# First stage on 64x64 quarters, third stage in halves, rows of x and of first-stage results moved as 48 + 48 + 2, and three buffers of third-stage results

## The chip, the cores and the metric

The kernel runs on one core of a Trainium2 chip. The metric is device time in microseconds of one execution. Five engines run side by side, each working its own list of instructions in order: TensorE (PE, with weight loads shown as PEld), VectorE (DVE), ScalarE (ACT), GpSimd (POOL) and SyncE (SP), which here issues all DMAs. They wait for each other by semaphores.

## The reference

```python
X = np.fft.rfft(x, axis=1)                    # x: (8, 3136, 256) f32
Yr = Xr @ w_r - Xi @ w_i + b_r                # Xr, Xi = X.real, X.imag; w: 256x256
Yi = Xr @ w_i + Xi @ w_r + b_i
Y = soft_threshold(Yr, 0.01) + 1j * soft_threshold(Yi, 0.01)
x = np.fft.irfft(Y, n=3136, axis=1)
h = np.maximum(x @ w_in, 0.0)                 # w_in: 256x1024
conv_out = sum(conv_w[k] * shifted(h, k - 1) for k in range(3))
out = (h * sigmoid(conv_out)) @ w_out         # w_out: 1024x256
```

The batch has 8 images of 3136 = 49 x 64 rows.

## The kernel before, in words

The transform of 3136 points is split into 49 times 64. **Stage 1** does the 49-point part: an item is a pair (image, jc), of which there are 8 x 8; `load_x` brings four columns j of 98 rows (49 rows n, and two halves h of the 64, interleaved) into a tile xr of 98x4x256, `stage1` multiplies by f1 (98x98, which holds the same 49-point table for both h) in two f32 matmuls of 512 columns (two half-items), ScalarE copies each from its one bank of PSUM (pool ps1) to a1, and a1 goes to the scratch sc1 in HBM as one DMA of 98 rows. `stage1_head` does the eight items of image 0 ahead of the loop, on tiles of their own (hx, ha). **Stage 2** loads a2 from sc1 (512 KB, `load_a2`) and does the 64-point part for four frequencies u at once; **mix** is the complex product with w_r, w_i, with each f32 operand split into two parts (hi, lo) of a faster type, three matmuls for one, 36 in all; **threshold** is the soft threshold, on ACT, DVE and POOL; **stage 3** is the inverse 64-point part, 12 matmuls into ps_s3, four frequencies in two banks (pool psa), copied by ScalarE in one instruction to z1 (two buffers) and stored to the scratch sc2.

One loop of 50 items (and three turns to drain) runs them as a pipeline: iteration `it` has stage 2 of item it, mix of it-1, threshold of it-2, stage 3 of it-3. The order within an iteration is written out by hand, under `manual_schedule`, for TensorE, VectorE and ScalarE: generators are advanced in turn by `some(generator, n)`. Half-items of stage 1 for the following images are let in by `one(k)` at four places of an iteration. How many is told by `due`, the running total after iteration it: 2, 5, 9, 13, 16, then three more each to 34 at it = 10, then 13 in five iterations until all 112 are done at it = 40. `back(n)` puts steps of a background job between (splitting the feed-forward weights). SP's order and the head are ordered by the compiler's own scheduler.

After the loop, **stage 4** (line 514) is the inverse 49-point part: blocks of 32 f32 matmuls on 64x64 quarters of TensorE's array, with z2 loaded from sc2 by two DMAs a block into three buffers, and results in the two buffers of psh, two banks each. Then follow `up` (line 533), the convolution and gate, and `down` (line 561).

PSUM has eight banks, in this order: ps1 one, ps2 two, psm three, psa two. The pool psh takes the first four again after the loop.

Names in a profile lose their trailing numbers: ps_s is any of ps_s1, ps_s2, ps_s3, ps_s4 (the line tells which), a is a1 or a2, z is z1 or z2, sc is sc1 or sc2.

Of the kernel before, what the change touches and what calls it, by code (L numbers as in the profile page):

```python
# [19 lines left out]
R = 49  # L20
# [15 lines left out]
def _tables():  # L36
# [8 lines left out]
    fwd1 = np.zeros((R, 2, 2 * R))  # L45
    for h in range(2):
        for uu in range(1, U + 1):
            for c in range(2):
                fwd1[:, h, (uu - 1) * 4 + c * 2 + h] = f[:, c, uu]
        fwd1[:, h, 4 * U + h] = f[:, 0, 0]  # L50
# [9 lines left out]
    for uu in range(U + 1):  # L60
# [32 lines left out]
        "fwd1": fwd1.reshape(2 * R, 2 * R).astype(np.float32),  # L93
# [7 lines left out]
def spectral_ffn_kernel(ctx: ExitStack, tc: tile.TileContext, x, w_r, w_i, b_r, b_i,  # L101
# [19 lines left out]
    with ExitStack() as ab:  # L121
# [7 lines left out]
        ps1 = ab.enter_context(tc.tile_pool(name="ps1", bufs=1, space=PSUM))  # L129
# [4 lines left out]
        f1 = c1.tile([K1, P], F32, name="f1")[:, 0:K1]  # L134
# [19 lines left out]
        def load_mix():  # L154

            raw = [stg.tile([P, NT, D], F32, name=f"wm_raw{k}", tag="raw", bufs=2) for k in range(2)]
            for k in range(2):
                ld = nc.sync.dma_start(raw[k], (w_r, w_i)[k].rearrange("(t p) e -> p t e", p=P))
            split(wmix_hi[:, :, 0, :], wmix_lo[:, :, 0, :], raw[1])
# [4 lines left out]
            return ld  # L164
# [77 lines left out]
        def load_x(pool, b, jc, parts=1, **kw):  # L242

            xr = pool.tile([K1, JC, D], F32, name="xr", **kw)
            xv = x[b].rearrange("(n j) d -> n j d", j=H)[:, jc * JC:(jc + 1) * JC, :]
            w = JC // parts
            for k in range(0, JC, w):
                ld = nc.sync.dma_start(xr[:, k:k + w, :], xv[:, k:k + w, :])
            return xr, ld

        def stage1(b, jc, xr):

            a1 = s1p.tile([K1, JC, D], F32, name="a1", bufs=3)
            for j in range(0, JC, 2):
                ps = ps1.tile([K1, 2, D], F32, name="ps_s1")
                nc.tensor.matmul(ps, f1, xr[:, j:j + 2, :], start=True, stop=True)  # L256
                nc.scalar.copy(a1[:, j:j + 2, :], ps)
                if j + 2 == JC:
                    nc.sync.dma_start(sc1[b][:, jc * JC:(jc + 1) * JC, :], a1)
                yield None  # L260

        def stage1_head(xs, b=0):

            with tc.tile_pool(name="ha", bufs=1, reuse_waits="tile") as ha:
                for jc, xr in enumerate(xs):
                    a1 = ha.tile([K1, JC, D], F32, name=f"ha{jc}")
                    for j in range(0, JC, 2):
                        k = (jc * 2 + j // 2) % 4
                        if k < 3:
                            ps = psm.tile([K1, 2, D], F32, name="ps_s1h", tag=f"ps_mx{k}")  # L270
                        else:
                            ps = ps1.tile([K1, 2, D], F32, name="ps_s1")
                        nc.tensor.matmul(ps, f1, xr[:, j:j + 2, :], start=True, stop=True)  # L273
                        if j:
                            nc.vector.tensor_copy(a1[:, j:j + 2, :], ps)
                        else:
                            nc.scalar.copy(a1[:, j:j + 2, :], ps)
                    st = nc.sync.dma_start(sc1[b][:, jc * JC:(jc + 1) * JC, :], a1)
            return st
# [73 lines left out]
        def stage3(b, g, s):  # L353

            sh, sl = s
            ps = psa.tile([KQ, UG, D], F32, name="ps_s3")
            for k in range(UG):
                u = g * UG + k if g < NG else U + k % 2
                for n, (lt, rh) in enumerate(((i1_hi, sh), (i1_hi, sl), (i1_lo, sh))):
                    nc.tensor.matmul(ps[:, k, :], lt[:, u, :], rh[:, k, :], start=(n == 0), stop=(n == 2))  # L360
            z1 = io.tile([KQ, UG, D], F32, name="z1", bufs=2)
            nc.scalar.copy(z1, ps)
# [64 lines left out]
        for it in range(n_it + 3):  # L427
# [28 lines left out]
            one(1)  # L456
# [175 lines left out]
```

## Time and profile before

| | us |
|---|---|
| three runs | 1737.77, 1741.54, 1738.86; median 1738.86 |
| the profiled execution | 1738.14 |
| its span on the core | 1736.3 |
| TensorE busy in the span | 1690.5 (97%) |
| VectorE, ScalarE, GpSimd busy | 1471.0, 1198.4, 118.6 |
| TensorE clock granted, mean | 0.985 of full |

The span is the stretch between the first and the last recorded instruction. A busy TensorE is not one at its peak: the record of a matmul reaches from its start to the end of its results, and neighbours overlap. Durations of matmuls are therefore read from start to start. `<-` after a row's time names what the engine waited for.

### The profile page before, as it was taken

Reading aid. Unit: us, or ns where it says so; the run is one execution under the profiler, and the core shown is the slowest. Engines: PE = TensorE matmul, PEld = TensorE weight load, DVE = VectorE, ACT = ScalarE, POOL = GpSimd, SP = SyncE. Lnnn points to the kernel's source line nnn. Section 1 sums busy time; section 2 is a strip of 40 time slices with the busy share of each in tenths; the row PEclk is TensorE's granted clock in tenths of the full one; section 3 lists DMA queues with packets and bytes.
Section 4 is the critical chain, followed back from the end, with each engine's and each line's share of the span. In section 5 each row is a group of like instructions: output and inputs, shape, how many; then the busy total and the mean of one; then the engine's idle time right before and its main releaser. Section 6 shows DMA issues by size and latency. Waiting matters only on the chain.

```text
span 1736.3 us, 35086 instructions
## 1 busy us (share of the span) xinstructions
PE 1690.5 (97%) x14944; PEld 1552.5 (89%) x14944; DVE 1471.0 (85%) x1757; ACT 1198.4 (69%) x1565; POOL 118.6 (7%) x54
## 2 busy tenths in 40 slices
PE   5999999999997999999999999999999999999999
PEld 2778888888986999999999999999999999999998
DVE  2788988898993988888888898888888888888887
ACT  2567677767663877777777677777777777777776
POOL 0122222222230000000000000000000000000000
PEclk7999999999996999999999999999999999999999
DMA  7877777667435110111111111111101111100001
GB/s 229 256 236 243 229 227 239 223 203 250 142 106 130 39 41 22 31 51 51 52 53 53 38 41 51 51 41 51 51 22 42 51 51 42 51 22 22 22 22 43
DMA packets 134604, 165.87 MB, mean 96 GB/s; under 512 B 9166, under 2 KB 112590, under 8 KB 134448
## 3 DMA queue, kind: packets, MB, share of 16 engines
q1 hardware_dynamic: 134448, 163.62, 30.7%
q8 instruction: 118, 1.93, 0.5%
q14 instruction: 38, 0.31, 0.1%
HBM read 86.01 MB, written 77.59 MB: 94 GB/s over the span
## 4 chain that ended last, share of the span: by engine, by line
PE 93%; DMA 4%; DVE 2%; issue 1%; ACT 1%; SPq 0%; DVEq 0%; ACTq 0%
PE acc L561 32%; PE ps_h L533 32%; PE ps_mx L328 11%; PE ps_s L256 5%; PE ps_s L300 5%; PE ps_s L514 4%; PE ps_s L360 3%; DMA z<-sc 1%; DMA wm_raw<-in_w_i_dram 1%; DMA t<-in_fwd_dram 1%; DVE v L336 0%; DMA sc<-a 0%; PE ps_s1h L273 0%; DMA xr<-in_x_dram 0%; DVE p L332 0%
## 5 line engine op out<-in xcount | busy, mean ns | idle before, releaser
L561 PE MATMUL acc<-wout,gh 128*128 128x256 f32 x3136 | 567.7, 281 | 1.5 <-ACT gh L547 1.5
L533 PE MATMUL ps_h<-yh,win 128*128 128x450 f32 x1792 | 550.4, 368 | 0.0
L542 DVE SCALAR_TENSOR_TENSOR c<-h,cw,c 128x896 f32<-128x896 f32 x448 | 513.4, 1148 | 26.7 <-ACT c L540 24.5
L561 PEld LDWEIGHTS acc<-wout,gh 128*128 128x128 f32 x3136 | 491.3, 188 | 10.4 <-ACT gh L547 1.9
L561 PE MATMUL acc<-wout,gl 128*128 128x256 f32 x1568 | 437.0, 280 | 0.0
L533 PEld LDWEIGHTS ps_h<-yh,win 128*128 128x128 f32 x1792 | 339.2, 189 | 25.8
L535 ACT ACTIVATE h<-ps_h 128x900 f32<-128x900 f32 x224 | 207.1, 925 | 209.9 <-PE ps_h L533 209.9
L533 PE MATMUL ps_h<-yl,win 128*128 128x450 f32 x896 | 329.7, 368 | 0.0
L544 DVE TENSOR_TENSOR c<-h,c 128x896 f32<-128x896 f32 x224 | 243.9, 1089 | 70.1 <-ACT c L543 69.6
L561 PEld LDWEIGHTS acc<-wout,gl 128*128 128x128 f32 x1568 | 293.6, 188 | 0.1
L548 DVE TENSOR_TENSOR gl<-c,gh 128x896 fp32r<-128x896 f32 x224 | 243.2, 1089 | 41.4 <-ACT gh L547 40.5
L547 ACT CAST gh<-c 128x896 fp32r<-128x896 f32 x224 | 211.6, 945 | 60.9 <-DVE c L544 60.5
L543 ACT ACTIVATE c<-c 128x896 f32<-128x896 f32 x224 | 214.0, 955 | 52.8 <-DVE c L542 51.8
L328 PE MATMUL ps_mx<-wmix_hi,fl 128*128 128x256 f32 x600 | 185.1, 308 | 2.7 <-DVE fl L310 2.7
L328 PE MATMUL ps_mx<-wmix_hi,fh 128*128 128x256 f32 x600 | 183.5, 306 | 0.7 <-DVE v L336 0.5
L533 PEld LDWEIGHTS ps_h<-yl,win 128*128 128x128 f32 x896 | 169.6, 189 | 11.1
L540 ACT ACTIVATE c<-h,cw 128x896 f32<-128x896 f32 x168 | 175.1, 1042 | 1.8
L328 PE MATMUL ps_mx<-wmix_lo,fh 128*128 128x256 f32 x600 | 168.4, 281 | 0.0
L350 POOL TENSOR_TENSOR sl<-v,sh 128x1024 fp32r<-128x1024 f32 x50 | 118.4, 2368 | 407.7 <-PE ps_s L360 249.0
L336 DVE TENSOR_TENSOR v<-ps_mx,p 64x512 f32<-64x512 f32 x200 | 137.4, 687 | 2.9
L300 PEld LDWEIGHTS ps_s<-t,a 128*128 128x128 f32 (+1 forms) x800 | 99.4, 197 | 37.0 <-issue 26.3
L328 PEld LDWEIGHTS ps_mx<-wmix_hi,fh 128*128 128x128 f32 x600 | 113.2, 189 | 19.1 <-issue 17.4
(84 smaller groups left out, 1861.0 us busy)
## 6 DMA issues: line engine op xcount, KB each, us to landing
z<-sc SPq DMA_DIRECT2D x128, 200.0 KB
xr<-in_x_dram SPq DMA_DIRECT2D x63, 392.0 KB
a<-sc SPq DMA_DIRECT2D x48, 512.0 KB
sc<-z SPq DMA_DIRECT2D x48, 512.0 KB
out_dram<-o SPq DMA_DIRECT2D x27, 896.0 KB
sc<-a SPq DMA_DIRECT2D x56, 392.0 KB
sc<-ha SPq DMA_DIRECT2D x8, 392.0 KB
win_bits<-in_moe_w_in_dram SPq DMA_DIRECT2D x4, 512.0 KB
```

Source lines behind the costliest of these rows:

```text
L300: nc.tensor.matmul(ps[:, k], a2[0:rows, k, t * P:(t + 1) * P], t2[0:rows, u, :], start=(k == 0), stop=(k == UG - 1), skip_group_check=True)
L328: nc.tensor.matmul(ps[c][:, k, :], lt, rh, start=(n == 0), stop=(n == len(mm) - 1))
L336: nc.vector.tensor_tensor(v[dst, :, k, :], ps[c][src], p1[src, c], op=ALU.add)
L533: nc.tensor.matmul(ps[:, a, 0:CH + 2], lt, rh, start=(n == 0), stop=(n == len(mm) - 1))
L535: nc.scalar.activation(h, ps[:, :, 0:CH + 2], AF.Relu)
L540: nc.scalar.mul(c, h[:, :, 0:CH], cw[:, 0, f:f + 1])
L542: nc.vector.scalar_tensor_tensor(c, h[:, :, k:k + CH], cw[:, k, f:f + 1], c, op0=ALU.mult, op1=ALU.add)
L543: nc.scalar.activation(c, c, AF.Sigmoid)
L544: nc.vector.tensor_tensor(c, h[:, :, 1:CH + 1], c, op=ALU.mult)
L547: nc.scalar.copy(gh, c)
L548: nc.vector.tensor_tensor(gl, c, gh.bitcast(F32), op=ALU.subtract)
L561: nc.tensor.matmul(acc[m // 2][:, m % 2, :], lt[:, sl], rh[:, f, :], start=(f == 0 and n == 0 and m % 2 == 0), stop=(f == NF - 1 and n == ...
```

## The change

- Stage 1 puts the two halves h at partitions 0 to 48 and 64 to 112, with f1 as one 49x64 table for each. An item is four f32 matmuls of 49x64 by 512 columns, one on each quarter of the array (row half h, output half c, where c picks two of the four columns j). The results of h go to a bank of their own (ps1 has two buffers).
- x is loaded as 48 + 48 + 2 rows of 4 KB, three DMAs; a1 is stored as three DMAs, in runs of 2 KB. f1 is loaded as 128x64.
- Whole items take the place of half-items: `due` becomes (due + 1) // 2, and there are two places for them, after the first eight matmuls of mix and at the end of the iteration.
- Stage 3 works two frequencies at a time into one bank (psa one bank), with a copy each; its first half stands amid mix, its second at the end. z1 has three buffers.
- The head's order is written out too: all items of image 0 come ahead of the splitting of the mixing weights.
- The scratch kept for descriptors of DMAs is set to 4096 bytes.

```diff
-        f1 = c1.tile([K1, P], F32, name="f1")[:, 0:K1]
+        f1 = c1.tile([P, P], F32, name="f1")[:, 0:SP]
-        ps1 = ab.enter_context(tc.tile_pool(name="ps1", bufs=1, space=PSUM))
+        ps1 = ab.enter_context(tc.tile_pool(name="ps1", bufs=2, space=PSUM))
...
+        def load_x(pool, b, jc, **kw):
+            xr = pool.tile([P, JC, D], F32, name="xr", **kw)
+            xv = x[b].rearrange("(n h j) d -> h n j d", h=2, j=H)[:, :, jc * JC:(jc + 1) * JC, :]
+            for h in range(2):
+                nc.sync.dma_start(xr[h * SP:h * SP + R - 1], xv[h, 0:R - 1])
+            ld = nc.sync.dma_start(xr[R - 1::SP], xv[:, R - 1])
+            return xr, ld
+        def quarters(ps, xr):
+            for c in range(2):
+                for h in range(2):
+                    rows = slice(h * SP, h * SP + R)
+                    nc.tensor.matmul(ps[h][c * SP:(c + 1) * SP], f1[rows, :], xr[rows, 2 * c:2 * c + 2, :], start=True, stop=True)
+        def store_a1(b, jc, a1):
+            to = sc1[b].rearrange("(w h) (q c j) d -> q c w h j d", h=2, c=2, j=2)[jc]
+            for c in range(2):
+                nc.sync.dma_start(to[c, 0:R - 1], a1[c * SP:c * SP + R - 1])
+            return nc.sync.dma_start(to[:, R - 1], a1[R - 1::SP])
         def stage1(b, jc, xr):
-            a1 = s1p.tile([K1, JC, D], F32, name="a1", bufs=3)
-            for j in range(0, JC, 2):
-                ps = ps1.tile([K1, 2, D], F32, name="ps_s1")
-                nc.tensor.matmul(ps, f1, xr[:, j:j + 2, :], start=True, stop=True)
-                nc.scalar.copy(a1[:, j:j + 2, :], ps)
-                if j + 2 == JC:
-                    nc.sync.dma_start(sc1[b][:, jc * JC:(jc + 1) * JC, :], a1)
-                yield None
+            a1 = s1p.tile([P, 2, JC // 2, D], F32, name="a1", bufs=3)
+            ps = [ps1.tile([P, JC // 2, D], F32, name="ps_s1") for h in range(2)]
+            quarters(ps, xr)
+            for h in range(2):
+                nc.scalar.copy(a1[:, h], ps[h])
+            store_a1(b, jc, a1)
+            yield None
...
         def stage3(b, g, s):
             sh, sl = s
-            ps = psa.tile([KQ, UG, D], F32, name="ps_s3")
-            for k in range(UG):
...
-            z1 = io.tile([KQ, UG, D], F32, name="z1", bufs=2)
-            nc.scalar.copy(z1, ps)
+            z1 = io.tile([KQ, UG, D], F32, name="z1", bufs=3)
+            for h in range(0, UG, 2):
+                ps = psa.tile([KQ, 2, D], F32, name="ps_s3")
+                for k in range(h, h + 2):
...
+                nc.scalar.copy(z1[:, h:h + 2, :], ps)
+                if h == 0:
+                    yield None
...
             with tc.issue_after(ld.ins):
-                load_mix()
+                mix_w = load_mix()
+                next(mix_w)
                 load_t2(0)
-                st = stage1_head(xh)
+                with tc.manual_schedule(engines={mybir.EngineType.PE, mybir.EngineType.DVE, mybir.EngineType.Activation}):
+                    st = stage1_head(xh)
+                    next(mix_w)
...
+            due = (due + 1) // 2
...
-            one(1)
+            one(0)
             some(two, 1)
             some(mx, 5)
...
-            some(mx, 5 if n_a > 3 else 9)
-            one(2)
+            some(mx, 9)
+            some(s3, 1)
             some(th, 1)
-            some(mx, 9)
-            one(3)
             some(mx, 64)
...
-            if 0 <= it - 3 < n_it:
-                stage3(*items[it - 3], ss.pop(it - 3))
-            one(0)
+            some(s3, 1)
+            one(1)
```

How TensorE's list changes, in the middle of the loop. Before, from the end of stage 3 to the first half-item inside mix (ps_mx is mix, ps_s at line 300 is stage 2):

```order
L360 MATMUL ps_s_2527<-sh,i_lo 128x256
L256 MATMUL ps_s_2543<-xr,f_113 98x512
L300 MATMUL ps_s_2552<-t_114,a_2435 128x128 x4
L300 MATMUL ps_s_2561<-t_114,a_2435 128x128 x4
L328 MATMUL ps_mx_2572<-wmix_hi,fh 128x256
L328 MATMUL ps_mx_2572<-wmix_lo,fh 128x256
L328 MATMUL ps_mx_2572<-wmix_hi,fl 128x256
L328 MATMUL ps_mx_2572<-wmix_hi,fh 128x256
L328 MATMUL ps_mx_2572<-wmix_lo,fh 128x256
L328 MATMUL ps_mx_2572<-wmix_hi,fl 128x256
L328 MATMUL ps_mx_2572<-wmix_hi,fh 128x256
L328 MATMUL ps_mx_2572<-wmix_lo,fh 128x256
```

Now, inside mix, from the last mixing matmuls ahead of an item to those behind it:

```order
L337 MATMUL ps_mx_2591<-wmix_hi,fh 128x256
L337 MATMUL ps_mx_2591<-wmix_lo,fh 128x256
L256 MATMUL ps_s_2612<-xr,f_113 64x512
L256 MATMUL ps_s_2613<-xr,f_113 64x512
L256 MATMUL ps_s_2612<-xr,f_113 64x512
L256 MATMUL ps_s_2613<-xr,f_113 64x512
L337 MATMUL ps_mx_2591<-wmix_hi,fl 128x256
```

An item is one group of four, the two h alternating, where single matmuls of 98 rows were spread over the iteration.

At the end of the loop, TensorE's list before, where stage 4 begins (line 514, two blocks interleaved; line 360 is stage 3):

```order
L360 MATMUL ps_s_5711<-sl,i_hi 128x256
L360 MATMUL ps_s_5711<-sh,i_lo 128x256
L360 MATMUL ps_s_5734<-sh,i_hi 128x256
L514 MATMUL ps_s_5817<-i_76,z_5814 64x49
L514 MATMUL ps_s_5855<-i_76,z_5852 64x49 x2
L514 MATMUL ps_s_5817<-i_76,z_5814 64x49
```

And now (stage 4 is line 529, stage 3 line 371, mix line 337):

```order
L337 MATMUL ps_mx_6064<-wmix_lo,fh 128x256
L337 MATMUL ps_mx_6064<-wmix_hi,fl 128x256
L529 MATMUL ps_s_6303<-i_76,z_6300 64x49
L529 MATMUL ps_s_6341<-i_76,z_6338 64x49 x2
L529 MATMUL ps_s_6303<-i_76,z_6300 64x49
L529 MATMUL ps_s_6341<-i_76,z_6338 64x49
```

The first two blocks of stage 4 moved from behind the last mix to ahead of it; the next two stand after 21 of its 36 matmuls, two more behind its end, and the others among the last halves of stage 3.

SP's list in the loop, before and now, for one item of stage 1 (z is z1, a<-sc the load of a2):

```order
L285 DMA a_1312<-sc_1_58 128x4x256
L248 DMA xr<-in_x_dram 98x1024
L259 DMA sc_2_59<-a_1077 98x1024
L248 DMA xr<-in_x_dram 98x1024
L364 DMA sc_0_65<-z_1191 128x1024
```

```order
L294 DMA a_1478<-sc_1_58 128x4x256
L247 DMA xr<-in_x_dram 48x1024 x2
L248 DMA xr<-in_x_dram 2x1024
L262 DMA sc_2_59<-a_1275 96x1x512 x2
L263 DMA sc_2_59<-a_1275 2x2x512
L376 DMA sc_0_65<-z_1306 128x1024
```

Each DMA on this list waits for the landing of the one eight places before it, since eight semaphores are used in turn, and otherwise for its source and target.

More of the change, by code (lines that the diff above doesn't have):

```diff
@@ L44, in _tables @@
     f[:, 1, :] = -np.sin(ang)
[L45 to L50, printed above, removed]
+    fwd1 = np.zeros((2, SP, SP))
+    for uu in range(1, U + 1):
+        for c in range(2):
+            fwd1[:, :R, (uu - 1) * 2 + c] = f[:, c, uu]
+    fwd1[:, :R, 2 * U] = f[:, 0, 0]
     g = np.transpose(f, (1, 2, 0)).copy()
@@ L158, in load_mix @@
                 ld = nc.sync.dma_start(raw[k], (w_r, w_i)[k].rearrange("(t p) e -> p t e", p=P))
+            yield ld
             split(wmix_hi[:, :, 0, :], wmix_lo[:, :, 0, :], raw[1])
@@ L240, in later @@
                 yield from work
[L242 to L248, printed above, removed]
-            return xr, ld
-        def stage1(b, jc, xr):
-            a1 = s1p.tile([K1, JC, D], F32, name="a1", bufs=3)
-            for j in range(0, JC, 2):
-                ps = ps1.tile([K1, 2, D], F32, name="ps_s1")
-                nc.tensor.matmul(ps, f1, xr[:, j:j + 2, :], start=True, stop=True)
-                nc.scalar.copy(a1[:, j:j + 2, :], ps)
-                if j + 2 == JC:
-                    nc.sync.dma_start(sc1[b][:, jc * JC:(jc + 1) * JC, :], a1)
-                yield None
+        def load_x(pool, b, jc, **kw):
[4 more added lines that the diff above has]
+            ld = nc.sync.dma_start(xr[R - 1::SP], xv[:, R - 1])
+            return xr, ld
+        def quarters(ps, xr):
[5 more added lines that the diff above has]
+            to = sc1[b].rearrange("(w h) (q c j) d -> q c w h j d", h=2, c=2, j=2)[jc]
+            for c in range(2):
+                nc.sync.dma_start(to[c, 0:R - 1], a1[c * SP:c * SP + R - 1])
+            return nc.sync.dma_start(to[:, R - 1], a1[R - 1::SP])
+        def stage1(b, jc, xr):
+            a1 = s1p.tile([P, 2, JC // 2, D], F32, name="a1", bufs=3)
[5 more added lines that the diff above has]
+            yield None
         def stage1_head(xs, b=0):
@@ L265, in stage1_head @@
                 for jc, xr in enumerate(xs):
[L266 to L278, printed above, removed]
+                    a1 = ha.tile([P, 2, JC // 2, D], F32, name=f"ha{jc}")
+                    if jc % 2:
+                        ps = [psm.tile([P, JC // 2, D], F32, name="ps_s1h", tag=f"ps_mx{h}") for h in range(2)]
+                    else:
+                        ps = [ps1.tile([P, JC // 2, D], F32, name="ps_s1") for h in range(2)]
+                    quarters(ps, xr)
+                    nc.scalar.copy(a1[:, 0], ps[0])
+                    nc.vector.tensor_copy(a1[:, 1], ps[1])
+                    st = store_a1(b, jc, a1)
             return st
@@ L355, in stage3 @@
             sh, sl = s
-            ps = psa.tile([KQ, UG, D], F32, name="ps_s3")
-            for k in range(UG):
-                u = g * UG + k if g < NG else U + k % 2
-                for n, (lt, rh) in enumerate(((i1_hi, sh), (i1_hi, sl), (i1_lo, sh))):
-                    nc.tensor.matmul(ps[:, k, :], lt[:, u, :], rh[:, k, :], start=(n == 0), stop=(n == 2))
-            z1 = io.tile([KQ, UG, D], F32, name="z1", bufs=2)
-            nc.scalar.copy(z1, ps)
+            z1 = io.tile([KQ, UG, D], F32, name="z1", bufs=3)
+            for h in range(0, UG, 2):
+                ps = psa.tile([KQ, 2, D], F32, name="ps_s3")
+                for k in range(h, h + 2):
+                    u = g * UG + k if g < NG else U + k % 2
+                    for n, (lt, rh) in enumerate(((i1_hi, sh), (i1_hi, sl), (i1_lo, sh))):
+                        nc.tensor.matmul(ps[:, k - h, :], lt[:, u, :], rh[:, k, :], start=(n == 0), stop=(n == 2))
+                nc.scalar.copy(z1[:, h:h + 2, :], ps)
+                if h == 0:
+                    yield None
             if g < NG:
@@ L367, in stage3 @@
                     nc.sync.dma_start(sc2[b + k][:, U, :], z1[:, k, :])
+            yield None
         def some(g, n):
@@ L431, in spectral_ffn_kernel @@
             due = (2, 5, 9, 13, 16)[it] if it < 5 else 16 + 3 * (it - 4) if it <= 10 else 34 + 13 * (it - 10) // 5
+            due = (due + 1) // 2
             n_a, given = due - given, due
+            s3 = stage3(*items[it - 3], ss.pop(it - 3)) if 0 <= it - 3 < n_it else iter(())
             work = 5 <= it < n_it
```

7 lines of the change are left out of this document (3 added, 4 removed).

## The prediction

> **What bounds the kernel now.** I read the engine totals and the chain first, then busy time by stage, then single iterations, then the matmuls of the changed lines one by one, last the transfers.
>
> ```profile
> PE 1690.5 (97%) x14944; PEld 1552.5 (89%) x14944; DVE 1471.0 (85%) x1757; ACT 1198.4 (69%) x1565; POOL 118.6 (7%) x54
> PE 93%; DMA 4%; DVE 2%; issue 1%; ACT 1%; SPq 0%; DVEq 0%; ACTq 0%
> ...
> 0.00:20.00 20.00, 12.84 (x24) 4.56 (x24) 3.57 (x8) 4.62 (x8) 0.20 (x4) 0.98 0.82 227
> ...
> 40.00:60.00 20.00, 15.33 (x87) 12.48 (x88) 10.02 (x18) 8.73 (x17) 0.00 (x0) 0.83 0.97 268
> ...
> 45.77:99.47 53.70, 51.24 (x330) 42.11 (x331) 40.31 (x66) 34.31 (x59) 9.41 (x4) 0.96 0.76 234
> 99.47:149.44 49.97, 49.97 (x350) 42.37 (x351) 41.20 (x73) 34.58 (x57) 10.06 (x5) 1.00 0.74 241
> 149.44:439.24 289.80, 289.80 (x2078) 249.88 (x2077) 256.14 (x422) 206.54 (x334) 70.84 (x31) 1.00 0.71 229
> 439.24:509.10 69.86, 67.75 (x565) 66.11 (x564) 67.96 (x116) 45.90 (x74) 20.95 (x9) 1.00 0.49 138
> 509.10:555.73 46.63, 31.40 (x726) 28.65 (x725) 20.88 (x30) 17.25 (x19) 7.14 (x3) 0.74 0.45 119
> 555.73:1736.30 1180.57, 1174.83 (x10850) 1112.60 (x10848) 1033.06 (x1033) 848.77 (x1005) 0.00 (x0) 1.00 0.14 41
> ```
>
> The windows are: stretch, length, then busy time of PE, PEld, DVE, ACT, POOL, the granted clock, the DMA share, GB/s. TensorE is the chain, but not everywhere. Until 45.77 us the kernel waits for transfers; from 99.47 to 439.24 TensorE never stops; from 439.24 to 509.10, with stage 1 over, VectorE is the fullest engine (67.96 of 69.86); from 509.10 to 555.73 both idle at a clock of 0.74. After 555.73 (stage 4 and the feed-forward part, 1180.57 us) nothing is edited, so the change must earn its time in the first third.
>
> One iteration each with two, three and no half-items of stage 1, and a late one:
>
> ```profile
> 168.57:177.69 9.12, 9.12 (x70) 8.10 (x68) 6.98 (x13) 6.32 (x11) 2.36 (x2) 1.00 0.78 225
> 177.69:187.70 10.01, 10.01 (x72) 8.49 (x70) 9.34 (x17) 7.43 (x13) 2.36 (x2) 1.00 0.76 256
> 439.24:446.63 7.39, 7.39 (x65) 7.39 (x64) 6.20 (x12) 4.11 (x8) 1.72 (x1) 1.00 0.47 142
> 495.23:502.88 7.65, 7.65 (x67) 7.53 (x65) 7.56 (x13) 5.15 (x8) 2.40 (x1) 1.00 0.18 71
> ```
>
> Without stage 1 an iteration is 7.39 us of TensorE; each half-item adds 0.87 ((9.12 - 7.39) / 2). The late one is VectorE's: it lasts 0.09 longer than its 7.56 busy.
>
> **The matmuls of stage 1.** Their records, and the place of one half-item among the mixing matmuls:
>
> ```profile
> L256 PE MATMUL ps_s<-xr,f x224: 590/592/1061, 38.3 to 438.8; 98*98 98x512 f32 x112
> ...
> 260.40 0.28 PE L328 MATMUL ps_mx<-wmix_hi,fl 128*128 128x256 f32 x1
> 260.52 1.02 PE L256 MATMUL ps_s<-xr,f 98*98 98x512 f32 x2
> 260.98 0.69 PE L328 MATMUL ps_mx<-wmix_hi,fh 128*128 128x256 f32 x1
> 261.50 0.28 PE L328 MATMUL ps_mx<-wmix_lo,fh 128*128 128x256 f32 x1
> ```
>
> An f32 matmul is two records. The next mixing matmul but one starts at 261.50 and mixing matmuls follow each other by 0.12, so the half-item holds TensorE from 260.52 to 261.38: 0.86 us, 0.43 a record, 1.72 for a whole item of two matmuls. The change replaces the two by four of 49x64 on quarters of the array, eight records of the same 512 columns. One after the other they would take 8 x 0.43 = 3.44. What quarters do side by side is seen in stage 4, which uses them already:
>
> ```profile
> 631.15 0.37 PE L533 MATMUL ps_h<-yl,win 128*128 128x450 f32 x1
> 631.36 0.37 PE L533 MATMUL ps_h<-yh,win 128*128 128x450 f32 x1
> 631.66 0.27 PE L514 MATMUL ps_s<-i,z 50*64 50x49 f32 x4
> ...
> 631.66 1.15 PE L514 MATMUL ps_s<-i,z 50*64 50x49 f32 x64
> 632.74 0.51 PE L561 MATMUL acc<-wout,gh 128*128 128x256 f32 x2
> 633.08 0.28 PE L561 MATMUL acc<-wout,gl 128*128 128x256 f32 x1
> ```
>
> The first four records of the block lie within 0.27 us, hardly more than one: they run together. 16 rounds of four take 1.15, so a round takes (1.15 - 0.27) / 15 = 0.059, where one record of 49 columns alone would take 0.041 (0.43 x 49 / 512): 0.018 over it. The whole block displaces TensorE from 631.57 (631.36 and a step of 0.21) to 632.85 (633.08 less two steps of 0.12): 1.28, of which 16 x 0.059 = 0.94 are rounds and 0.34 are spent on entering and leaving the quarters. So an item becomes 2 x (0.43 + 0.018) + 0.34 = 1.24, a saving of 0.48. Bounds: if all of the 1.28 above four-fold overlap (0.66) were fixed, 0.86 + 0.62 = 1.48; if all of it grew with the columns, 1.28 / 64 x 512 / 49 x 8 = 1.67; if only the row halves overlap, 4 x 0.43 + 0.34 = 2.06. I take 1.24, since the block's rows give both parts separately.
>
> The Trainium skill speaks against the change here: "TensorEngine Tiling (Array Packing)", Tiling Modes, says that changing the tiling mode drains TensorE, and stage 1 now does so twice an item, where 98x98 did it never. The block's 0.34 agrees. "TensorE: Matmul & The Clock Gate", Part 3, has packed matmuls span one duration and some 4 ns for each further tile; by that alone an item would be an estimated 0.88 and the sum below some 14 us lower, with VectorE then the bound.
>
> **The sum, stage by stage.**
>
> Iterations 11 to 40 (149.44 to 439.24) hold 30 x 7.39 = 221.7 of other work and 39 items. With 1.24 each that is 270.1, against 289.8: -19.7. VectorE's 256.1 are not edited, so its share rises from 88% to 95%; by the late iteration the last engine costs about 0.1 an iteration in hand-overs, and I give back 3.5. Net -16. Iterations 6 to 10 (99.47 to 149.44): 5 x 7.39 + 7 x 1.24 = 45.6 for 49.97, hand-overs 0.3: -4.
>
> ```profile
> L257 ACT COPY a<-ps_s x112: 571/587/624, 40.0 to 439.5; 98x512 f32<-98x512 f32 x112
> ...
> L362 ACT COPY z<-ps_s x50: 996/1012/1020, 76.4 to 534.5; 128x1024 f32<-128x1024 f32 x50
> ```
>
> ScalarE still copies two times 512 columns an item, and stage 3 in halves two of 0.587 instead of 1.012, +0.16 an iteration on an engine that is busy 206.5 of 289.8: free. Its price if the cover goes: the second half's matmuls wait for the first half's copy in the one bank. Between the halves stand 15 mixing matmuls, 1.75 us, against 0.587. The third z1 buffer takes away a wait nobody shows: 0.
>
> **The transfers.** Rows of the head and of iteration 5:
>
> ```profile
> 1.25 5.02 SPq L248 DMA_DIRECT2D xr<-in_x_dram x9
> ...
> 7.40 11.78 DMA wm_raw<-in_w_i_dram
> ...
> 27.56 2.91 DMA sc<-ha
> 34.03 11.61 DMA t<-in_fwd_dram
> ...
> 88.07 7.37 DMA sc<-a
> 95.46 3.87 DMA a<-sc
> ```
>
> In the head 9 issues become 24: at 0.56 each 13.4 us of SP's queue, ahead of the mixing weights. That would be bad if ScalarE's head copies still stood behind the weights' split (the chain waits for wm_raw until 19.18); the written-out order puts all eight copies ahead of it. What then ends the head is the bytes: 0.82 busy at 227 GB/s, where 0.97 and 268 are possible. Gain up to 4; but the second table load (34.03 to 45.64) comes after six further x loads on SP, loss up to 2. I take -1.5. Iterations 1 to 5 (53.7 us, 2.4 of them idle behind sc<-a and a<-sc at 88 to 99): TensorE's work falls to 5 x 7.39 + 9 x 1.24 = 48.1, and the last item of the second image moves from the end of iteration 4 to its first third, which takes that wait away; the transfers there are near their limit, so I take -3.5 of the 5.6.
>
> The Trainium skill, "DMA: Bandwidth & Descriptors", section "Why a DMA increments its semaphore by 16 and not by 1", says a DMA runs on the largest number of engines up to 16 that divides its rows: 14 for 98, 16 for 48. A share of 0.82, below 14/16, agrees; by the rule alone the head's loads and stores would shrink by an eighth, an estimated 3 us instead of my 1.5.
>
> In iterations 6 to 40 SP issues some 9.8 DMAs each instead of 4.6; at 0.34 to 0.56 that is 3.3 to 5.5 us of 9.0 and hidden. Bytes are the same, so the rate rises from 229 to some 246 GB/s, below the 268.
>
> **The passage to stage 4.**
>
> ```profile
> 519.76 0.38 PE L360 MATMUL ps_s<-sh,i_hi 128*128 128x256 f32 x1 [1.43 <-ACT z L362]
> 520.08 2.19 PE L514 MATMUL ps_s<-i,z 50*64 50x49 f32 x128
> ...
> 523.08 5.38 DMA z<-sc
> ...
> 549.32 4.49 DMA z<-sc
> ...
> 555.80 6.32 PE ps_h L533 x24
> ```
>
> Here ten blocks of stage 4 go in pairs: load, compute, load, and the feed-forward part starts at 555.80. The first pair runs at 520.08, behind the last mixing. Afterwards it stands ahead of the last mixing, whose place now is 510.8: the four banks it needs are free earlier because stage 1 has two banks of its own and stage 3 one. The next loads start about 10 us earlier and run beside the mixing and stage 3. But TensorE takes its work in order, and half of the last mixing then stands behind the second pair's load. Between 0 and -11 I take -8, near the shift, since the loads are the chain there.
>
> Sum: -16 - 4 - 3.5 - 1.5 - 8 = -33 against the profiled execution's 1738.1 (1736.3 of span; the median of the runs is 0.7 above): **1705 us**.
>
> **Rivals.**
> 1. Slower: SP's queue becomes the bound. Each DMA waits for the one eight places before it on the queue. 9.8 an iteration and 8 under way allow a mean landing of 8 x 9.0 / 9.8 = 7.3 us; sc<-a took 7.37. At 8.5 an iteration lasts 10.4, 35 iterations lose 26 us against today, and the rest (-13) does not cover it: 1751. It turns slower from about 8.2. Against it: smaller DMAs land sooner, and the engines are at 0.71. 6%.
> 2. Slower: columns of the array do not overlap for 512 different columns on the same rows (in stage 4 both column halves stream the same i2). 2.06 an item, +0.34 x 56 = +19, the head and the passage give -9.5: 1748. Against it: 64 records in 1.15. 6%.
> 3. The overhead grows with columns, 1.67 an item: 56 x 0.05 and the -10.5 of head, early wait and passage: 1725. 9%.
> 4. VectorE takes over: its iterations range from 6.98 to 9.34, TensorE's would be 8.63 or 9.87, and if they do not average out, 9.35 an iteration leaves -9 of the -16: 1712. 13%.
> 5. The passage gives nothing or costs 3, TensorE standing before z loads: 1713 to 1716. 15%.
> 6. As forecast, 1698 to 1712: 51%.
>
> The range 1697 to 1726 takes in 3 to 6 with 88% less their edges. Within 0.2% (3.5 us, about what a measurement tells from no change) lies little: between case 3 and the slower two, 3%. Slower 11%, faster 86%.
>
> **What would show it.** Stage 1's records in groups of four, two groups 0.44 apart, and 1.2 us from the mixing matmul before to the one after; iterations of 8.6 and 9.9 us; VectorE 95% busy there with waits of TensorE on it under 0.2 us; iteration 6 starting near 94 instead of 99.47; the first ps_h of the feed-forward part 30 us earlier than 555.80. I am wrong if the groups of four follow each other singly, if waits of stage 2 on a<-sc or of stage 1 on xr appear between 100 and 400 us, or if the last mixing is torn by a wait for z<-sc longer than what its earlier start gained.

## The result and the profile after

The changed kernel takes 1712.69 us (median of four runs, 1711.09 to 1716.76) against 1738.32 us (1735.23 to 1741.54) for the kernel before: ratio 0.9856, 95% interval 0.983 to 0.9882. It is faster by 1.4%, with the interval below 1, and 7.7 us short of the 1705 forecast. The profiled execution took 1713.93 us with a span of 1712.2, 24.1 less than the 1736.3 before.

The page's engine totals and chain, then the same stretches of the program as were shown of before (columns as there; the first two rows are the two halves of the head):

```profile
PE 1661.2 (97%) x15200; PEld 1527.2 (89%) x15200; DVE 1471.0 (86%) x1757; ACT 1206.8 (70%) x1615; POOL 119.2 (7%) x54
...
PE 91%; DVE 1%; DMA 1%; ACT 0%; issue 0%; POOL 0%; SPq 0%; DVEq 0%; POOLq 0%; ACTq 0%
```

```profile
0.00:20.00 20.00, 14.15 (x60) 3.45 (x64) 4.42 (x9) 5.22 (x9) 0.20 (x4) 1.00 0.89 210
20.00:40.00 20.00, 2.46 (x13) 1.03 (x6) 4.58 (x7) 2.71 (x5) 0.00 (x0) 1.00 0.74 207
49.59:99.37 49.78, 47.22 (x369) 38.65 (x369) 40.70 (x66) 34.83 (x63) 9.19 (x4) 0.96 0.86 242
99.37:144.92 45.55, 45.55 (x376) 38.95 (x377) 38.52 (x71) 35.35 (x61) 9.78 (x5) 1.00 0.90 271
144.92:414.73 269.81, 269.81 (x2234) 232.70 (x2233) 256.34 (x422) 211.87 (x362) 71.25 (x30) 1.00 0.82 249
414.73:486.31 71.58, 69.75 (x572) 67.06 (x570) 70.79 (x120) 48.33 (x84) 21.62 (x9) 1.00 0.42 130
486.31:530.92 44.61, 32.85 (x720) 29.61 (x719) 20.08 (x29) 17.12 (x22) 7.12 (x3) 0.70 0.56 140
530.92:1712.20 1181.28, 1175.40 (x10848) 1112.89 (x10848) 1032.87 (x1033) 848.04 (x1004) 0.00 (x0) 1.00 0.14 41
```

| stretch | before, us | after, us | measured | forecast |
|---|---|---|---|---|
| head, to stage 2 of iteration 1 | 45.77 | 49.59 | +3.8 | -1.5 |
| iterations 1 to 5 | 53.70 | 49.78 | -3.9 | -3.5 |
| iterations 6 to 10 | 49.97 | 45.55 | -4.4 | -4 |
| iterations 11 to 40 | 289.80 | 269.81 | -20.0 | -16 |
| iteration 41 to the end of the last mix but one | 69.86 | 71.58 | +1.7 | 0 |
| from there to the first row of stage 5 (line 548, the `up` of the feed-forward part) | 46.63 | 44.61 | -2.0 | -8 |
| the rest | 1180.57 | 1181.28 | +0.7 | 0 |
| sum | 1736.3 | 1712.2 | -24.1 | -33 |

The whole gain arose in the loop (-28.3 us in its first three rows). Head and passage, which were to give 9.5 us, cost 3.5 together, the row above the passage counted in. Three iterations after, with one item, two and none, and the records around one item:

```profile
144.92:153.54 8.62, 8.62 (x74) 7.67 (x73) 8.52 (x16) 6.69 (x12) 2.38 (x1) 1.00 1.04 343
153.54:163.27 9.73, 9.73 (x83) 7.84 (x81) 8.86 (x17) 7.18 (x12) 3.27 (x2) 1.00 0.96 303
414.73:422.18 7.45, 7.45 (x66) 7.45 (x65) 7.36 (x13) 4.96 (x10) 2.37 (x1) 1.00 0.49 153
```

```profile
246.33 0.28 PE L337 MATMUL ps_mx<-wmix_lo,fh 128*128 128x256 f32 x1
246.54 1.09 PE L256 MATMUL ps_s<-xr,f 49*64 49x512 f32 x8
247.56 0.38 PE L337 MATMUL ps_mx<-wmix_hi,fl 128*128 128x256 f32 x1
247.78 0.28 PE L337 MATMUL ps_mx<-wmix_hi,fh 128*128 128x256 f32 x1
```

The mixing matmul before ends its turn at 246.45 (246.33 and a step of 0.12); the second one behind starts at 247.78, one step after 247.66. The item holds TensorE for 1.21 us, where it held it for 1.72. The eight records share a row because they overlap: two groups of four, starting at 246.54 and 247.02. The three iterations agree: each item adds 1.14 to 1.17 us to the 7.45 of the one without.

### The profile page after: what moved, and what is told of

Read it like the earlier page. It is cut to its first block, busy times and chain, and to the rows that moved or that the text cites. A ratio compares the mean times of both kernels' runs of the same rounds, so it can differ in the third digit from the quotient of the medians.

```text
span 1712.2 us, 35834 instructions
## 1 busy us (share of the span) xinstructions
PE 1661.2 (97%) x15200; PEld 1527.2 (89%) x15200; DVE 1471.0 (86%) x1757; ACT 1206.8 (70%) x1615; POOL 119.2 (7%) x54
## 4 chain that ended last, share of the span: by engine, by line
PE 91%; DVE 1%; DMA 1%; ACT 0%; issue 0%; POOL 0%; SPq 0%; DVEq 0%; POOLq 0%; ACTq 0%
PE acc L576 33%; PE ps_h L548 32%; PE ps_mx L337 10%; PE ps_s L309 4%; PE ps_s L529 4%; PE ps_s L371 4%; PE ps_s L256 3%; DMA z<-sc 1%; DVE v L345 0%; POOL sl L359 0%; DMA sc<-z 0%; DVE v L356 0%; ACT sh L358 0%; DVE yl L536 0%; DVE p L341 0%
## 5 line engine op out<-in xcount | busy, mean ns | idle before, releaser
L576 PEld LDWEIGHTS acc<-wout,gh 128*128 128x128 f32 x3136 | 491.2, 188 | 10.4 <-ACT gh L562 1.9
L337 PE MATMUL ps_mx<-wmix_hi,fh 128*128 128x256 f32 x600 | 172.7, 288 | 0.5 <-DVE v L345 0.5
L337 PE MATMUL ps_mx<-wmix_hi,fl 128*128 128x256 f32 x600 | 172.4, 287 | 0.5 <-DVE fl L319 0.4
L337 PEld LDWEIGHTS ps_mx<-wmix_hi,fl 128*128 128x128 f32 x600 | 113.3, 189 | 33.6 <-issue 32.5
```

Source lines behind the costliest of these rows:

```text
L337: nc.tensor.matmul(ps[c][:, k, :], lt, rh, start=(n == 0), stop=(n == len(mm) - 1))
L576: nc.tensor.matmul(acc[m // 2][:, m % 2, :], lt[:, sl], rh[:, f, :], start=(f == 0 and n == 0 and m % 2 == 0), stop=(f == NF - 1 and n == ...
```

## The experiments

The twelve runs below are told by what they settle. Times are medians, and the ratio behind a time is to the kernel before in runs on the same chip, where that took 1737.62 to 1738.56 us; differences between two runs below can be from two chips. The changed kernel was run once more, beside two z1 buffers, the second run of both edits and six z2 buffers: 1712.85 us, 0.9857 (0.9843 to 0.987), iterations 11 to 40 again 269.81, stage 2 of iteration 1 at 49.65.

> The changed kernel itself, on the chip of the three beside it, as their base: 1711 to 1716, 0.984 to 0.987 of the kernel before.

### The quarters alone: stage 1 put back on the whole array

```diff
-                for h in range(2):
-                    rows = slice(h * SP, h * SP + R)
-                    nc.tensor.matmul(ps[h][c * SP:(c + 1) * SP], f1[rows, :], xr[rows, 2 * c:2 * c + 2, :], start=True, stop=True)
+                nc.tensor.matmul(ps[c], f1, xr[:, 2 * c:2 * c + 2, :], start=True, stop=True)
```

The table f1, the loads and the stores take the layout of before (98 adjoining partitions), in DMAs of 48 + 48 + 2 rows.

> The changed kernel with stage 1 put back on the whole array: two 98x98 matmuls of 512 columns with the table of before, results stored in runs of 4 KB; the three DMAs of 48 + 48 + 2 rows, the order of the loop and stage 3 in halves stay. Theory (the overlap of the quarters is the gain): an item takes 1.72 us of TensorE again instead of 1.22, so iterations 11 to 40, with 39 items, go from 269.8 to about 289 us and the whole from 1712.7 to 1735 to 1741. Rival (the gain comes from the order, the smaller tiles of stage 3 or the DMAs): iterations 11 to 40 stay within 3 us of 269.8 and the whole at 1709 to 1716. On the head, beside it: if the 0.6 us that SyncE takes to issue a store came from the 1 KB pieces of the new layout, these issues fall back to 0.3 us and the first stage 2 of iteration 1 comes about 6 us earlier than 49.6; if they come from the number of rows or of DMAs, it stays at 49 to 50.

Measured: 1735.13 us, 0.9979 (0.9969 to 0.9988). The window of iterations 11 to 40 and the records of one item:

```profile
145.86:434.99 289.13, 289.13 (x2079) 248.44 (x2078) 257.50 (x422) 213.58 (x362) 71.21 (x30) 1.00 0.74 229
```

```profile
245.10 0.28 PE L336 MATMUL ps_mx<-wmix_lo,fh 128*128 128x256 f32 x1
245.22 1.88 PE L255 MATMUL ps_s<-xr,f 98*98 98x512 f32 x4
246.53 0.68 PE L336 MATMUL ps_mx<-wmix_hi,fl 128*128 128x256 f32 x1
247.05 0.28 PE L336 MATMUL ps_mx<-wmix_hi,fh 128*128 128x256 f32 x1
```

The item is back at 1.71 us (245.22 to 246.93, by steps of 0.12), and 39 items make 19.3 us in the window (289.13 - 269.81). The medians differ by 22.4 (1735.13 - 1712.69), the profiled spans by 19.8 (1732.0 - 1712.2): the quarters are most of the gain (25.6 by the medians, 24.1 by the spans), and that is what is left of them after the head's loss, for here stage 2 of iteration 1 came at 45.17, 4.4 earlier than after (about 6 was expected), with the same 24 loads and 24 stores. The rest, 3.2 us at 0.9979, belongs to what this kernel keeps of the change: the order, the halves and the split of the rows.

### What a round costs and what the switch costs: the quarters twice

```diff
             quarters(ps, xr)
+            quarters(ps, xr)
             for h in range(2):
                 nc.scalar.copy(a1[:, h], ps[h])
```

> The changed kernel with the eight quarter matmuls of an item issued twice, one set of eight right behind the other, in the loop (the head is left as it is). Theory (an item is two rounds of 0.43 to 0.45 us and 0.34 us for going to quarters and back): a doubled item is two rounds longer, 0.87 to 0.9 us, so 1.22 goes to 2.1 us, and 56 items add 48 to 51 us: 1760 to 1764 in all, iterations 11 to 40 at 303 to 305 us. Rival (there is no price for going to quarters and back; each round is 0.6 us): 1.22 goes to 2.43 us and 56 items add 67 us: 1780. Rival (the four quarters of a round do not overlap in full, the time hangs on the moving data): starts of a group of four more than 0.5 us behind those of the group before.

Measured: 1760.17 us, 1.0123 (1.0104 to 1.0141); iterations 11 to 40:

```profile
156.28:460.12 303.84, 303.84 (x2547) 245.21 (x2546) 257.50 (x422) 213.12 (x362) 71.24 (x30) 1.00 0.74 219
```

34.0 us more for 39 items: 0.873 for two rounds, so a round is 0.436, hardly more than one record of 512 columns on the whole array (0.43). The rest of the 1.21, 0.34 us, is paid once an item however many rounds it has: going to the quarters and back. The rival of 0.6 a round would have given 317 in this window.

### Stage 3 in halves and the third z1 buffer

Halves alone, in the kernel before (stage 1 as it was, its freed bank of PSUM used):

```diff
-            ps = psa.tile([KQ, UG, D], F32, name="ps_s3")
-            for k in range(UG):
...
+            z1 = io.tile([KQ, UG, D], F32, name="z1", bufs=3)
+            for h in range(0, UG, 2):
+                ps = psa.tile([KQ, 2, D], F32, name="ps_s3")
```

> The kernel before with stage 3 in halves alone: one PSUM bank for each half, the freed banks as second buffer of stage 1, three buffers of third-stage results and the halves at the places of the changed kernel; stage 1 on the whole array with the table, loads and stores of before. Theory (nearly all of the 25.6 us belongs to stage 1 on quarters): iterations 11 to 40 stay within 3 us of the 289.8 before, the passage from the last mix of image group A to the first row of stage 5 changes by 2 us or less, the whole is 1733 to 1739. Rival (the halves bring a good part by freeing PSUM and spreading ScalarE's copies): iterations 11 to 40 at 280 or less and the whole at 1728 or less.

Measured: 1736.28 us, 0.9991 (0.9981 to 1.0001).

```profile
148.61:438.40 289.79, 289.79 (x2077) 249.86 (x2076) 256.47 (x422) 213.69 (x363) 70.88 (x31) 1.00 0.71 229
```

289.79 against 289.80: nothing in the loop, and about 2 us in all, at the edge of what the interval shows. The third buffer, taken back in the changed kernel:

```diff
-            z1 = io.tile([KQ, UG, D], F32, name="z1", bufs=3)
+            z1 = io.tile([KQ, UG, D], F32, name="z1", bufs=2)
```

> The changed kernel with two buffers of third-stage results instead of three. Theory (the store of z1 lands long before the buffer is wanted again, an iteration of 8.6 to 9.7 us later, so the third buffer takes away a wait that is not there): within 2 us of the changed kernel. Rival (with the store now competing with three times as many transfers on the queue, ScalarE's copy of the first half waits for it and holds the copies behind it): iterations 11 to 40 go from 269.8 to 275 or more.

Measured: 1713.26 us, 0.986 (0.9847 to 0.9873), iterations 11 to 40 at 269.81 again. It is worth nothing that can be measured.

### The split of the rows

```diff
             for h in range(2):
-                nc.sync.dma_start(xr[h * SP:h * SP + R - 1], xv[h, 0:R - 1])
-            ld = nc.sync.dma_start(xr[R - 1::SP], xv[:, R - 1])
+                ld = nc.sync.dma_start(xr[h * SP:h * SP + R], xv[h])
```

The stores likewise: two of 49 rows.

> The changed kernel with the rows of x and of first-stage results moved in two DMAs of 49 rows instead of three of 48, 48 and 2. Theory (what the head lost is SyncE's time to issue: 24 loads and 24 stores instead of 16 and 16 of this form): the first stage 2 of iteration 1 comes 4 to 6 us earlier than 49.6, the loop is unchanged, the whole is 1707 to 1710. Rival (the number of rows sets over how many DMA engines a transfer is spread, so that 49 rows are carried by far fewer than 48): the 16 loads of the head, 3.2 MB, take about 29 us at 7 of 16 engines instead of 15, the head is 15 us or more longer, the loop's loads and stores of 31 MB at 109 GB/s become its bound, and the whole is 1740 to 1870.

Measured: 1773.37 us, 1.0198 (1.0183 to 1.0213): the theory was wrong and the rival right in its way and its range, though the head lost 13.4 us, not 15 or more, and the loop ran at 221 GB/s, not at 109. Windows of the head's first 20 us and of iterations 11 to 40:

```profile
0.00:20.00 20.00, 14.87 (x49) 3.83 (x50) 3.55 (x7) 4.42 (x7) 0.20 (x4) 1.00 0.50 164
...
168.20:474.37 306.17, 290.06 (x2235) 241.88 (x2234) 257.24 (x423) 211.58 (x363) 71.19 (x30) 0.96 0.66 221
```

In the same stretch ScalarE's copies wait for the stores that free a1 (sum, times, longest):

```profile
ACT a L270 <- DMA sc<-a: 28.2, 11, 4.7
```

With the same bytes in fewer DMAs, the DMA share in the first 20 us falls from 0.89 to 0.50 and the rate from 210 to 164 GB/s; stage 2 of iteration 1 comes at 62.97 instead of 49.59, and the loop loses 36.4 us. TensorE is idle for 16.1 of them, 12.6 of these ahead of stage 1, waiting for x; the rest lies in its busy time, at a mean granted clock of 0.96 instead of 1.00. The Trainium skill, "DMA: Bandwidth & Descriptors", section "Why a DMA increments its semaphore by 16 and not by 1", has a transfer run on the largest number of engines up to 16 that divides its rows, which is 7 for 49 and 16 for 48; a share of 0.50, with some transfers of other shapes in it, agrees. So the split into 48 + 48 + 2 is what makes the partition layout of the quarters affordable. By itself it is hardly a gain: with whole-array matmuls and stage 3 in halves it gave 1735.13 beside the 1736.28 of 98 rows, and these two kernels differ in the head's order and in whole or half items as well.

### The head

A piece is an item of image 0, of which the head has eight. SyncE's issues of one piece's stores, and of the first load of a2 behind all of them, in the changed kernel (start, duration, line, tiles; x2 are two issues):

```profile
23.19 1.20 SPq L262 DMA_DIRECT2D sc<-ha  x2
24.44 0.53 SPq L263 DMA_DIRECT2D sc<-ha  x1
...
34.56 0.37 SPq L294 DMA_DIRECT2D a<-sc  x1
```

and in the kernel with stage 1 on the whole array, with as many DMAs of as many rows:

```profile
22.82 0.77 SPq L261 DMA_DIRECT2D sc<-ha  x2
23.63 0.31 SPq L262 DMA_DIRECT2D sc<-ha  x1
...
30.27 0.38 SPq L293 DMA_DIRECT2D a<-sc  x1
```

A 48-row store takes 0.60 us to issue where its rows go out as two pieces of 2 KB, and 0.39 with one piece of 4 KB (the expectation of 0.3 was too low); the two-row store 0.53 with its rows 64 partitions apart and in pieces of 2 KB, and 0.31 with whole rows side by side. The distance of the partitions counts by itself: two-row loads, whole rows in both kernels, take 0.49 and 0.24. (The expectations call the pieces 1 KB by mistake.) In the changed kernel SyncE issues without a pause from 17.38 to 32.5: the queue is the bound there. What is lost up to the first load of a2 is what the head loses: stage 2 of iteration 1 starts 15.0 us behind the issue of that load before (30.74) and after (34.56), and 14.7 to 15.0 behind it in the three other kernels of this section. Two tests took work off the queue.

```diff
+                    xa = hx.tile([P, H, D], F32, name="xa")
+                    nc.sync.dma_start(xa[R - 1::SP], xv[:, R - 1])
...
+                for c in range(2):
+                    st = nc.sync.dma_start(to[c, R - 1].rearrange("h q j d -> q h (j d)"), aa[c * SP + R - 1:c * SP + R].rearrange("p q h j d -> p q h (j d)"))
```

> The changed kernel where, in the head alone, row 48 of both halves comes in one load for all eight pieces and goes out in two stores at the end: 17 loads and 18 stores instead of 24 and 24. In the trace SyncE spends 1.89 us on the three stores of a piece, 0.53 of it on the one of two rows, and 0.50 us on each load of two rows. Theory (SyncE's time to issue sets the head): six stores of 0.53 us fewer bring the first stage-2 load and with it stage 2 of iteration 1 from 49.6 to 46 us, and the loads of x, which go at the pace of their bytes, do not move; the whole is 1709 to 1710. Rival (the bytes set it, 3.2 MB in and 3.2 MB out at 207 to 210 GB/s are 15 us each): it stays at 49 to 50. Rival (the single big load of row 48 comes first and puts off the first piece): it goes to 50 to 52.

Measured: 1712.35 us, 0.9854 (0.9838 to 0.9871), stage 2 of iteration 1 at 47.70: half of the step expected, and nothing of it to be told apart in the whole. SyncE still spent 14.0 us on these stores (17.49 to 31.53): many of the 48-row ones took longer than 0.60, up to 0.99, and the two gathered ones 0.72 each, so that 1.1 us were saved of the 3.2 that six issues of 0.53 make. Then the same transfers on two queues:

```diff
+            q = q2 or nc.sync
+            nc.sync.dma_start(to[0, 0:R - 1], a1[0:R - 1])
+            q.dma_start(to[1, 0:R - 1], a1[SP:SP + R - 1])
...
-                    st = store_a1(b, jc, a1)
+                    st = store_a1(b, jc, a1, nc.scalar)
```

> The changed kernel where, in the head alone, one of the two 48-row stores of each piece is issued by ScalarE's queue instead of SyncE's; the transfers themselves are the same. Theory (SyncE's time to issue stores of this layout, 0.60 to 0.67 us each, sets the head): SyncE's part of a piece falls from 1.89 to about 1.2 us, eight pieces take 9.6 instead of 15.1 us, the first stage 2 of iteration 1 comes 4 to 5 us earlier than 49.6, and the whole is 1707 to 1709. Rival (the 1 KB pieces are slow in the DMA engines themselves, and SyncE only waits for room): it stays at 49 to 50 and the stores take longer from issue to landing by what the issue became shorter.

Measured: 1709.96 us, 0.9839 (0.9822 to 0.9855); stage 2 of iteration 1 at 46.39, 3.2 earlier, somewhat under the 4 to 5 expected. (One of the four executions took 4308 us, and nothing here explains it; the median of the other three is 1709.83. The 13 executions of the later kernels with this edit had none like it.) The queues' rows, SyncE's and ScalarE's:

```profile
26.08 0.63 SPq L262 DMA_DIRECT2D sc<-ha  x1
26.75 1.01 SPq L264 DMA_DIRECT2D sc<-ha  x1
...
31.70 0.38 SPq L295 DMA_DIRECT2D a<-sc  x1
```

```profile
26.46 0.58 ACT L286 COPY ha<-ps_s1h 128x512 f32<-128x512 f32 x1 [0.93 <-PE ps_s1h L256]
27.27 0.56 ACTq L263 DMA_DIRECT2D sc<-ha  x1
```

The issue of a2 moves from 34.56 to 31.70; the pace now hangs in part on ScalarE's copies, which wait for TensorE between their DMAs. The head's loss is SyncE's time to issue stores of this shape, shown by both kernels that shorten it with all bytes kept; it is not the number of issues, which is the same on the whole array.

### The passage to stage 4

The window of the passage, in two parts that meet where VectorE has finished the last block of image 0, which is all that the first row of stage 5 needs; first before, then after:

```profile
509.10:551.81 42.71, 28.19 (x630) 25.70 (x632) 19.90 (x29) 16.34 (x18) 7.14 (x3) 0.76 0.42 115
551.81:555.73 3.92, 3.21 (x108) 2.95 (x102) 0.98 (x2) 0.91 (x1) 0.00 (x0) 0.50 0.75 159
```

```profile
486.31:517.01 30.70, 23.81 (x599) 22.07 (x598) 18.92 (x23) 13.43 (x17) 4.77 (x2) 0.79 0.52 125
517.01:530.92 13.91, 9.04 (x127) 7.55 (x122) 1.16 (x7) 3.69 (x6) 2.35 (x1) 0.50 0.66 174
```

The earlier start came as forecast, and this part of the passage is 12.0 us shorter; 10.0 were given back behind it. What VectorE waits for there, after:

```profile
515.15 1.86 DVE L536 TENSOR_TENSOR yl<-ps_s,yh 128x784 fp32r<-128x784 f32 x2 [3.79 <-ACT yh L535]
525.60 0.06 DVE L512 MEMSET yh<- 128x2 f32 x1 [8.59 <-PE ps_s L371]
525.63 0.06 DVE L513 MEMSET yh<- 128x2 f32 x1
529.86 0.06 DVE L512 MEMSET yl<- 128x2 f32 x1 [4.17 <-DMA sc<-z]
```

Two columns of image 1's buffers are cleared on memory that the loop's last tiles hold. These clears wait for the last stage 3 and then for its store to land, and in VectorE's and TensorE's lists two blocks of image 1 stand behind them, ahead of the first row of stage 5. Before, the last store was earlier against the blocks, and the same wait lay amid image 0's, whose loads went on meanwhile:

```profile
540.90 0.06 DVE L497 MEMSET yl<- 128x2 f32 x1 [6.25 <-DMA sc<-z]
```

The test lets image 1 begin behind the second row:

```diff
-    ys[1] = new_y(1)
-    for jg in range(2):
-        stage4(1, jg, ys[1])
-    todo = [(1, jg) for jg in range(2, NPC)]
+    todo = []
...
+            if st == 1:
+                ys[1] = new_y(1)
+                todo = [(1, jg) for jg in range(NPC)]
```

> The changed kernel where the buffers of image 1 and the stage-4 blocks that fill them start behind the second row of stage 5 instead of ahead of the first; all else as it was. Theory (in the passage VectorE's queue stands at clearing a column of image 1's buffer until the last store of third-stage results has landed at 529.6, and so holds back the row of stage 5 that would be ready at about 516): the first row of stage 5 comes 10 to 15 us earlier than 530.9, some of that is given back as VectorE then waits behind it with less done, and the whole is 1701 to 1708. Rival (the passage is set by the eight loads of second-stage pieces, 5.7 us each, and by the last stage 3, and the wait only fills it): the first row comes earlier but the rows behind it later by as much, and the whole stays at 1711 to 1715.

Measured: 1706.0 us, 0.9817 (0.9803 to 0.9832), 6.9 less than the changed kernel's 1712.85, which ran on another chip; the two ratios, 0.9817 and 0.9857, say the same.

```profile
525.37 0.69 DVE L553 TENSOR_SCALAR c<-h,cw 128x896 f32<-128x896 f32 x1 [10.08 <-ACT h L550]
...
528.36 0.06 DVE L512 MEMSET yl<- 128x2 f32 x1
```

The wait on the store is gone from the clears. The first row comes at 514.46, 16.5 earlier; the profiled span is 9.2 shorter (1703.0), so 7.3 are given back behind it, where VectorE now waits 10.08 us for the h of the first row (4.66 in the changed kernel), which shares TensorE with the last stage 3.

### A version faster than both

Both edits together, run twice, then with six z2 buffers in place of three.

> The two edits together: one 48-row store of each head piece issued by ScalarE's queue, and image 1's buffers and stage-4 blocks behind the second row of stage 5. Theory: the two lie in places that do not touch, so their gains add, 4 to 5 us in the head and 5 to 11 us in the passage: 1697 to 1704. Rival (the loop's start is set by what else the queue must load there, so that a shorter head only makes iteration 1 to 5 wait longer): the passage's gain alone, 1701 to 1708.

> The kernel with one 48-row store of each head piece on ScalarE's queue and image 1's stage 4 behind the second row of stage 5, timed beside the changed kernel: 9 to 12 us less than it, 1700 to 1704.

Measured: 1702.47 us, 0.9796 (0.9781 to 0.9811), and 1703.16, 0.9803 (0.9789 to 0.9816). The gains add: 2.9 and 6.9 make 9.8, and 1712.85 less 1703.16 is 9.7.

```diff
-    zio, y_a = pool("zio", 3), pool("y_a")
+    zio, y_a = pool("zio", 6), pool("y_a")
```

> The kernel of both edits with six buffers of second-stage pieces (z2) instead of three; with them the order of TensorE also puts the second pair of stage-4 blocks behind the whole last mix instead of into it. Theory (with image 1 out of the way, the passage is set by the loads of these pieces, which go in turns of 4.6 to 5.8 us because three buffers let no more be under way, and by the last mix standing behind the second pair): the first row of stage 5 comes 6 to 12 us earlier than 512.3, about half of it is left at the end, and the whole is 1695 to 1699. Rival (the last stage 3 and VectorE's thresholds ahead of it, 38.7 us behind the last mix of group A, set the passage whatever the loads do): the first row earlier by 3 us or less and the whole at 1700 to 1704. Rival (the six buffers lie on memory that the loop frees late, and so the first loads start later): a longer passage, 1704 to 1710.

Measured: 1697.11 us (1694.95 to 1699.19), 0.9765 (0.9752 to 0.9779): the fastest, 15.7 us under the changed kernel. Its way was another than expected. The first row of stage 5 came at 510.55, only 1.8 to 4.8 earlier than in the two runs of both edits (512.30, 515.35), and about 4.8 more were won behind it (1184.9 from there to the end against 1189.7), where the granted clock was higher too: 0.92 in the first 29.45 us against 0.81. The window from the end of the last mix but one to the first row, then TensorE's rows of its last three pairs of blocks and of the first row:

```profile
485.61:510.55 24.94, 21.81 (x453) 19.99 (x451) 14.53 (x23) 13.78 (x18) 7.15 (x3) 0.68 0.59 160
...
493.66 3.32 PE L530 MATMUL ps_s<-i,z 50*64 50x49 f32 x128 [0.17 <-DVE yl L537]
498.96 3.77 PE L530 MATMUL ps_s<-i,z 50*64 50x49 f32 x128 [0.62 <-DVE yl L537]
504.72 3.83 PE L530 MATMUL ps_s<-i,z 50*64 50x49 f32 x128 [0.41 <-DVE yl L537]
510.55 0.74 PE L549 MATMUL ps_h<-yh,win 128*128 128x450 f32 x1 [0.41 <-DVE yl L537]
```

No pair waits for a load any more (4.1 us in all in the first run of both edits). What sets their pace of 5.3 to 5.8 us is the hand-over of the two buffers of PSUM: TensorE (3.3 to 3.8), ScalarE's copy (0.90), VectorE's subtraction (0.99). TensorE's part is long because of the clock, which was 0.65 around the first of these pairs and 0.50 around the other two; in the changed kernel a pair at 486.31, at a clock of 1.00, took 2.19 us. So the loads were one limit with another close behind it. The first rival had the small step of the first row right, but not the total, and its limit, the last stage 3 and the thresholds, is not the one that these rows show. Six buffers and the other order of TensorE came in one edit; this run does not tell them apart.

## Why the prediction was right, and where it was not

The direction, the cause (the item on quarters) and the range of 1697 to 1726 were right; the time is 0.7 us beyond the 1698 to 1712 of case 6. That it came so near owes something to luck, since two errors went opposite ways: by the rows of the table the loop gave 4.8 us more than forecast, and everything else 13.7 less.

- **The item.** 1.24 us forecast, 1.21 measured, with both parts near what stage 4's block gave: rounds of 0.436 (0.448 forecast), 0.34 for the switch. The rule of the Trainium skill on the switch ("TensorEngine Tiling (Array Packing)", Tiling Modes) agrees with a price paid once a visit; that a drain is what takes the 0.34 no run here shows. By the 4 ns a tile alone of the Trainium skill's "TensorE: Matmul & The Clock Gate", Part 3, the item would be an estimated 0.88; the trace has 1.21, so these 4 ns are not the whole price.
- **Iterations 11 to 40.** The sum of TensorE's work, 270.1, was right to 0.3 us. Wrong was the term that gave 3.5 us back for hand-overs as VectorE nears its limit: TensorE was never idle, and waited for nothing, with VectorE busy 256.34 of 269.81. Rival 4's time of 1712 is met, its mechanism is not.
- **Iterations 1 to 10.** -7.5 forecast, -8.3 measured. In iterations 1 to 5 the mechanism was partly another: the wait behind sc<-a and a<-sc went, as forecast, but TensorE's idle time did not shrink (2.46 before, 2.56 after). Now it waits 1.0 for x at 72.29 and 1.5 for VectorE ahead of iteration 6; the gain is the 4.0 us of shorter work.
- **The head** is a mis-sized term: -1.5 forecast, +3.8 measured, outside its stated -4 to +2. The step that failed was to count the queue's work for the 24 loads alone and let the bytes end the head. The loads' 13.4 us came true (1.20 to 14.65); the 24 stores were not priced at all, and with the 0.60 and 0.53 of their shape they hold SyncE for another 15.1 us.
- **The passage** is the other: -8 forecast, -2.0 measured. The loads did start earlier as said, and image 0 was ready 12 us sooner. The step left out was what is late next: the last stage 3 and its store, which image 1's buffers wait for, and which stand ahead of the first row. Rival 5 had the passage at nothing, and with it 1713 to 1716, by another way, the torn mix.
- **The row above it** (+1.7) was forecast at 0. Of it 0.8 lies inside that mix, where stage 3's first half, six matmuls, now stands. The other 0.9 arises between iteration 41 and the start of the last mix but one, which take 66.25 us here, 66.25 with whole-array stage 1, 65.88 with halves alone and 65.34 before. So it does not come from the shorter item and VectorE's fuller loop; how the halves and the edits beside them bring it stays open.
- **Rivals 1, 2 and 3** (SyncE's queue in the loop, columns that do not overlap, overhead growing with columns) have nothing left: TensorE is never idle in iterations 6 to 40, and a round takes 0.436. (In rival 1, 35 iterations of 10.4 us lose 25 us against before, not 26; nothing hangs on it.)

## What to carry to other kernels

A matmul that fills a quarter of TensorE's array is worth packing even at a switch for each item, if the price of the switch is read from a block that already does it: rounds and switch, measured apart elsewhere in the same trace, gave this item to 0.03 us. Where a stage's end is moved earlier, ask what else stands in the queues ahead of the next stage's first instruction; here the clearing of two columns, 0.06 us of work, held the first row back for some 14 us, of which 6.9 were won by moving it. Price the issue of a DMA by one of the same shape, not by another in the same queue.

## What the runs showed of the hardware that was not expected

- The time to issue a DMA followed its shape: 0.56 us for 98 rows of 4 KB, 0.39 for 48 rows of 4 KB, 0.60 for 48 rows of two 2 KB pieces, 0.23 to 0.31 for most DMAs of two adjoining rows, 0.49 to 0.55 for most of two rows 64 partitions apart.
- One row more, 49 for 48, with the same bytes: the busy share of the DMA engines fell from 0.89 to 0.50 in the first 20 us, and the loop lost 36 us.
- In the passage the granted clock fell to 0.50, and a pair of stage-4 blocks then took 3.8 us instead of the 2.19 at 1.00.
- With VectorE busy 95% of the 269.8 us of iterations 11 to 40, TensorE was busy through all of them.
